# Seven block products for units 2 to 7 of a first expert stage, and another way to turn float64 words into float32

## The chip, the cores and the metric

The kernel runs on one core of a Trainium2 chip. A core has TensorE for matrix products, VectorE, ScalarE and GpSimd for work on elements, and SyncE, which issues most transfers. The profile calls them PE (its weight loads PEld), DVE, ACT, POOL and SP. The metric is device time in microseconds (us), the median of several runs.

## The reference, cut to what matters

Attention with a bias of position gives 1152 tokens of 512 features. A feed-forward stage with softplus follows, and then a stage of eight experts, each weighted by a column of P, a matrix that is balanced eight times by rows and columns.

```
x = attention(q, k, v, w1, b1, w2)              # 1152 x 512
h = x @ w_in                                    # 512 x 2048
g = max(h, 0) + log1p(exp(-abs(h)))             # softplus
x = g @ w_out                                   # 2048 x 512
P = exp(x @ w_gate - max); 8 times: rows, columns normalised
for e in range(8):
    out += P[:, e:e+1] * (max(x @ w1[e], 0) @ w2[e])   # 512 x 1024, 1024 x 512
```

`w_in` and `w_out` come as float64, the other inputs as float32.

## The kernel before, in words

**Stages.** First the bias is built, then attention runs (to about 262 us of the profile), and then `experts` handles both expert stages as 40 units of 256 hidden columns. Units 0 to 7 (U1 = 8) are the softplus stage, called the first expert stage here. Units 8 to 39 are the eight experts, four units each. Tokens are cut into two chunks of 512 and a rest of 128 (CHUNKS). Each float32 operand is split into a high part (rounded to the type that TensorE multiplies, by ScalarE) and a low part (source minus high, by VectorE or GpSimd), and each product is three products, high with high, high with low, low with high (TRIPS). In the text the low part is called a low.

**A unit.** Up products make h for chunk c and half f of the hidden columns, h(c,f). A *plain* unit makes four of them, each with four slices of the 512 features, 12 matmuls, 48 in all (`plain`). A unit with *seven block products* takes the two chunks by two halves of the features as a 2 x 2 matrix of blocks A11 to A22, the weights as another, and makes the four results from seven products of sums of blocks (PRODUCTS: S1 to S4 are sums of token blocks, T1 to T4 of weight blocks), six matmuls each, 42 in all (`product`). The products are accumulated in three PSUM banks X, Y and Z (tags t, tail, pv); between products the banks are copied to SBUF (v1, u2, u3, by `keep` on ScalarE) and added (`add` on VectorE). The T blocks are mixed from the weights by `mix`, four subtractions on GpSimd (L633 to L636). The order of the products is UP = 1, 2, 6, 5, 7, 3, 4, and last the rest of the tokens (`up_last`). Before the change units 0 to 8 are plain and units 9 to 39 use seven products.

After the up products come softplus or relu and the split of h, then `down(u, 0)` and `down(u, 1)`, four groups of six matmuls each into two PSUM tiles `sum` of two banks (the groups 0 and 2 share one tile, 1 and 3 the other), `turn_last` (two transposes and a split, hl) and `down_last`, six matmuls for the rest of the tokens into bank pv. Each group is added into acc by `evac` (L835 on VectorE; in unit 0 a copy by ScalarE, L833). acc takes the same SBUF places as the tokens xr of the first stage.

**Weights.** A unit has four pieces of 128 x 512 words: k = 0, 1 of `w_in`, k = 2, 3 of `w_out`. Those of units 0 to 7 are float64 and are turned into float32 while the unit before runs: `m` (mask on VectorE, L604, clamp on GpSimd, L605, a tensor_scalar with max and min), `a` (shift and mask, L610), `b` (or in the bits of the low word, L615) and `c` (or in the sign, L621), the last three on VectorE. `high` and `highd` split the finished weights into wu and wd (ScalarE L639, 1024 columns, GpSimd L640). A list of steps CONVERT, written by hand, sets the order; `convert(n)` takes the next n steps of it, two after each up product and one after each group of down. The pieces of units 0 and 1 are loaded, and those of unit 0 converted, during attention (EARLY).

**Order.** Nothing is scheduled: each engine executes its instructions in the order of the program text, and waits at one hold up all behind it on that engine. Ahead of unit 0, `x_part` splits the last block A22 (L662 on ScalarE, L663 on GpSimd and VectorE) and `x_last` splits the rest of the tokens (xl). In unit 8, which is plain, the logits of the gate are made in bank pv (`logits`) and turned into rows there (`tokens_down`), with `gate` as the table of what is asked for at which point.

## Time and profile before

| | us |
|---|---|
| median of three runs | 1245.1 (1243.65 to 1245.86) |
| the profiled execution | 1242.65 |
| its span | 1240.9 |
| PE busy | 1187.5 (96%) |
| DVE busy | 758.0 (61%) |
| POOL busy | 553.9 (45%) |
| ACT busy | 530.3 (43%) |
| share of PE in the chain that ended last | 81% |
| share of DVE in that chain | 10% |

The busy time of TensorE is the share of the span in which a matmul was in the pipeline. The chain that ended last is followed back from the last instruction; 81% of it is TensorE, so most of what is saved or added there shows in the time. Times in the rows are from the start of the span. A row of a timeline has start, duration, engine, line, operation and result<-operands, and in brackets how long the engine was idle before it and for whom it waited.

### The profile page before, as it was taken

What the parts mean: (1) busy time and instruction counts of PE and PEld (TensorE: products, weight loads), DVE (VectorE), ACT (ScalarE), POOL (GpSimd) and SP (SyncE); (2) the same over time, 40 slices, a digit from 0 to 9 for tenths busy, and PEclk for the clock granted to TensorE, in tenths of its full rate; (3) what the DMA queues carried; (4) which work ended last, traced back from release to release, by engine and by line L of the source; (5) the groups of instructions that cost most, each with busy time, mean ns of one, the idle gap of its engine ahead of it and who ended that gap; (6) DMA issues with size and microseconds to landing.
All of it is one profiled execution on the core that took longest, in us unless ns stands there. A gap on an engine that the chain in (4) does not pass through costs nothing.

```text
span 1240.9 us, 18958 instructions
## 1 busy us (share of the span) xinstructions
PE 1187.5 (96%) x7454; PEld 1003.3 (81%) x7454; DVE 758.0 (61%) x1393; ACT 530.3 (43%) x923; POOL 553.9 (45%) x424
## 2 busy tenths in 40 slices
PE   5877899999999999999999999999999999999998
PEld 4776788878788887888888888888888888888887
DVE  8985778746776757466554554554554554555554
ACT  7976676765223334423523323323323423422421
POOL 0115677655445544534543543543543453453440
PEclk9898999999999999999999999999999999999999
DMA  3577565312222310101111111110111111111102
GB/s 102 170 209 202 169 193 167 94 35 85 85 86 85 102 53 33 52 35 35 52 51 35 51 51 34 52 52 35 51 51 34 52 52 35 51 51 35 34 1 77
DMA packets 58572, 90.85 MB, mean 73 GB/s; under 512 B 6900, under 2 KB 37236, under 8 KB 58484
## 3 DMA queue, kind: packets, MB, share of 16 engines
q1 hardware_dynamic: 58196, 89.35, 22.9%
q8 instruction: 58, 0.95, 0.3%
q10 hardware_dynamic: 288, 0.30, 0.1%
q14 instruction: 30, 0.25, 0.1%
HBM read 74.45 MB, written 15.19 MB: 72 GB/s over the span
## 4 chain that ended last, share of the span: by engine, by line
PE 81%; DVE 10%; ACT 3%; POOL 3%; DMA 2%; issue 2%; SPq 0%; POOLq 0%; DVEq 0%; ACTq 0%
PE sum L802 34%; PE t L705 14%; PE pv L705 7%; PE pv L818 4%; PE t L721 4%; PE tail L776 4%; PE tail L705 3%; PE op L474 3%; PE sps L386 2%; PE pv L721 2%; PE tail L721 2%; PE tp L437 2%; ACT m L199 1%; DVE m L202 1%; DVE f L610 1%
## 5 line engine op out<-in xcount | busy, mean ns | idle before, releaser
L640 POOL TENSOR_TENSOR wu<-f,wu 128x1024 fp32r<-128x1024 f32 x71 | 170.6, 2403 | 436.0 <-ACT wu L639 436.0
L802 PE MATMUL sum<-wd,h 128*128 128x512 f32 x1536 | 364.9, 393 | 0.0
L802 PEld LDWEIGHTS sum<-wd,h 128*128 128x128 f32 x1536 | 283.3, 188 | 56.1
L837 DVE SCALAR_TENSOR_TENSOR acc<-sum,prob,acc 128x512 f32<-128x512 f32 x224 | 168.2, 751 | 146.7 <-PE sum L802 146.7
L705 PE MATMUL t<-room,wu 128*128 128x512 f32 x496 | 137.8, 389 | 0.0
L731 ACT ACTIVATE v<-t 128x512 f32<-128x512 f32 x31 | 18.5, 597 | 232.7 <-PE t L705 232.7
L640 POOL TENSOR_TENSOR wd<-f,wd 128x1024 fp32r<-128x1024 f32 x40 | 96.2, 2406 | 40.8 <-ACT wd L639 32.6
L705 PEld LDWEIGHTS t<-room,wu 128*128 128x128 f32 x496 | 93.1, 188 | 19.5
L802 PE MATMUL sum<-h,wd 128*128 128x512 f32 x384 | 93.9, 397 | 1.7 <-DVE acc L835 1.0
L705 PE MATMUL pv<-x,wu 128*128 128x512 f32 x372 | 94.8, 390 | 0.0
L212 PE MATMUL pac<-bw,m 128*128 128x64 bf16 (+1 forms) x1920 | 69.3, 201 | 26.4 <-ACT m L199 13.4
L212 PEld LDWEIGHTS <-m 128*128 128x128 bf16 (+1 forms) x1920 | 66.0, 107 | 29.6 <-issue 16.9
L802 PEld LDWEIGHTS sum<-h,wd 128*128 128x128 f32 x384 | 69.9, 188 | 20.5 <-DVE acc L835 5.8
L639 ACT ACTIVATE wu<-f 128x1024 fp32r<-128x1024 f32 x71 | 74.7, 1053 | 15.3 <-DVE f L621 15.3
L705 PEld LDWEIGHTS pv<-x,wu 128*128 128x128 f32 x372 | 69.6, 188 | 14.4
L747 ACT ACTIVATE hl<-tail 128x256 fp32r<-128x256 f32 x40 | 15.3, 383 | 143.7 <-PE tail L785 143.7
L605 POOL TENSOR_SCALAR f<-f 128x512 f32<-128x512 f32 x32 | 61.6, 1934 | 27.8 <-DVE f L604 27.3
L705 PE MATMUL t<-x,wu 128*128 128x512 f32 x248 | 71.3, 389 | 0.0
L835 DVE TENSOR_TENSOR acc<-sum,acc 128x512 f32<-128x512 f32 x80 | 55.0, 688 | 24.3 <-PE sum L802 23.5
L403 ACT ACTIVATE p<-p,sm 128x576 f32<-128x576 f32 x72 | 55.6, 773 | 21.6 <-DVE sm L399 17.7
L726 DVE TENSOR_TENSOR tail<-tail,v 128x512 f32<-128x512 f32 x31 | 21.7, 699 | 68.7 <-PE tail L705 68.7
L639 ACT ACTIVATE wd<-f 128x1024 fp32r<-128x1024 f32 x40 | 42.1, 1053 | 47.4 <-DVE f L621 47.4
(197 smaller groups left out, 2121.8 us busy)
## 6 DMA issues: line engine op xcount, KB each, us to landing
f<-in_e_w_dram SPq DMA_DIRECT2D x128, 256.0 KB, 2.8
bias<-wt SPq DMA_DIRECT2D x16, 576.0 KB, 5.8
raw<-in_w_in_dram SPq DMA_DIRECT2D x16, 512.0 KB, 3.6
raw<-in_w_out_dram SPq DMA_DIRECT2D x16, 512.0 KB, 3.6
wt<-extra SPq DMA_DIRECT2D x10, 512.0 KB, 4.6
raw<-in_qT_dram SPq DMA_DIRECT2D x16, 288.0 KB, 4.4
raw<-in_kT_dram SPq DMA_DIRECT2D x16, 288.0 KB, 4.4
vr<-in_vN_dram SPq DMA_DIRECT2D x8, 448.0 KB, 4.9
```

Source lines behind the costliest of these rows:

```text
L212: nc.tensor.matmul(pt[0:n, g], lhs, win(w, (k * (ng + 1) + gw) * NC, [[(ng - gw) * NC, 2], [1, NC]]), start=(k == 0), stop=(k == 2))
L403: nc.scalar.activation(p, p, AF.Exp, bias=sm[:, o:o + 1], scale=-1.0, accum_out=sm[:, 2 + o:3 + o])
L605: nc.gpsimd.tensor_scalar(t, t, F64_MIN, F64_MAX, ALU.max, ALU.min)
L639: nc.scalar.activation(w[:, 0], src, AF.Copy)
L640: nc.gpsimd.tensor_tensor(out=w[:, 1], in0=src, in1=w[:, 0].bitcast(F32), op=ALU.subtract)
L705: nc.tensor.matmul(zz, wu(u)[:, a, o:o + 128], xs[xn][b][j], start=(n in (1, 2, 5) and k == 0), stop=(k == 5), skip_group_check=True)
L721: nc.tensor.matmul(zz, wu(u)[:, a, o:o + 128], xs[f"A{c + 1}{k // 2 + 1}"][b][k % 2], start=(k == 0 and n == 0), stop=(k == 3 and n == 2))
L776: nc.tensor.matmul(zr[:, 0:256], xl[:, b, k], wu(u)[:, a, 256 * k:256 * k + 256], start=(n == 0), stop=(n == 3 * KT - 1))
L802: nc.tensor.matmul(s, lhs, rhs, start=(n == 0), stop=(n == 5))
L818: nc.tensor.matmul(r, t[:, b, 128 * f:128 * f + 128], w[:, a, f], start=(n == 0), stop=(n == 5))
L835: nc.vector.tensor_tensor(out=d, in0=o, in1=d, op=ALU.add)
L837: nc.vector.scalar_tensor_tensor(out=d, in0=o, scalar=pool["prob"][:, t, e:e + 1], in1=d, op0=ALU.mult, op1=ALU.add)
```

## The change

Units 2 to 7 use seven block products (PLAIN). Their h goes through SBUF: `add` writes v1, u2 or u3, softplus is made in place on ScalarE, and three of four lows are GpSimd subtractions, held back until the product after next for two of them (`held`). The T blocks need `mix` and a second `high` for each of these units, which CONVERT now holds; `highd` is made in its own unit, after the fourth product. S1 to S4 are made in unit 0 on VectorE (`first_sum`, eight additions) and split in units 0 and 1 (`first_split`). The conversion steps of unit 1 move from unit 0's up products to its down products.

Step `m` becomes two scalings by powers of two, one on ScalarE (`rescale`, L602 after) and two multiplications on GpSimd (L603); the masks of steps `a` and `c` change by a bit. Both lows of A22 are made on VectorE. `tokens_down` uses bank tail, and three entries of `gate` are asked for one step later.

```diff
-        PLAIN = tuple(range(U1 + 1))
+        PLAIN = (0, 1, U1)
...
 
-        def magnitude(u, k):
+        def rescale(u, k):
 
             if u < U1 and wide:
                 t = whole(u, k)
-                nc.vector.tensor_scalar(t.bitcast(I32), words(u, k)[:, :, 1], 0x7FFFFFFF, None, ALU.bitwise_and)
-                nc.gpsimd.tensor_scalar(t, t, F64_MIN, F64_MAX, ALU.max, ALU.min)
+                nc.scalar.activation(t, words(u, k)[:, :, 1].bitcast(F32), AF.Copy, scale=2.0**111)
+                nc.gpsimd.tensor_scalar(t, t, 2.0**-112, 2.0**-111, ALU.mult, ALU.mult)
 
         def convert_a(u, k):
             if u < U1 and wide:
                 t = whole(u, k).bitcast(I32)
-                nc.vector.tensor_scalar(t, t, 3, 0x3FFFFFFF, ALU.logical_shift_left, ALU.bitwise_and)
+                nc.vector.tensor_scalar(t, t, 3, 0x7FFFFFFF, ALU.logical_shift_left, ALU.bitwise_and)
 
         def convert_b(u, k):
             if u < U1 and wide:
@@ -618,7 +616,7 @@
         def convert_c(u, k):
             if u < U1 and wide:
                 t, w = whole(u, k).bitcast(I32), words(u, k)
-                nc.vector.scalar_tensor_tensor(out=t, in0=w[:, :, 1], scalar=-0x40000000, in1=t, op0=ALU.bitwise_and,
+                nc.vector.scalar_tensor_tensor(out=t, in0=w[:, :, 1], scalar=-0x80000000, in1=t, op0=ALU.bitwise_and,
                                                op1=ALU.bitwise_or)
 
...
-        def add(bank_, name):
-            out = hold[name if name == "u3" else bank_]
+        def add(u, bank_, name):
+            out = hold[bank_ if u >= U1 and name != "u3" else name]
             nc.vector.tensor_tensor(out=out, in0=hold[bank_], in1=hold[name], op=ALU.add)
             return out
...
-        def split_h(u, t, src):
+        def split_h(u, t, src, eng=None):
             nc.scalar.activation(t[:, 0], src, AF.Copy if u < U1 else AF.Relu)
-            if u < U1:
+            if eng:
+                eng.tensor_tensor(out=t[:, 1], in0=src, in1=t[:, 0].bitcast(F32), op=ALU.subtract)
+            elif u < U1:
                 lows.append(lambda: nc.vector.tensor_tensor(out=t[:, 1], in0=src, in1=t[:, 0].bitcast(F32), op=ALU.subtract))
             else:
...
-            while held:
-                held.pop(0)()
+            if n in (6, 4):
+                while held:
+                    held.pop(0)()
             if n in (2, 7, 3, 4):
                 c, f = {2: (0, 0), 7: (1, 1), 3: (0, 1), 4: (1, 0)}[n]
-                z[c, f] = hold["X"] if n == 4 else add(*{2: ("Y", "v1"), 7: ("X", "u3"), 3: ("Z", "u2")}[n])
+                z[c, f] = hold["X"] if n == 4 else add(u, *{2: ("Y", "v1"), 7: ("X", "u3"), 3: ("Z", "u2")}[n])
                 low()
-                act(u, c, f, z[c, f])
+                if u >= U1:
+                    act(u, c, f, z[c, f])
+                    return
+                if n == 4:
+                    z[c, f] = pool["moe"].tile([128, 512], F32, tag="s3", bufs=1, name="s3")
+                t = h[c, f] = pool["moe"].tile([128, 2, 512], F32R, tag="h", bufs=4, name="h")
+
+                def rest_of():
+                    nc.scalar.activation(z[c, f], hold["X"] if n == 4 else z[c, f], AF.Softplus)
+                    split_h(u, t, z[c, f], None if n == 3 else nc.gpsimd)
+
+                if n in (2, 7):
+                    held.append(rest_of)
+                else:
+                    rest_of()
                 return
...
-                convert(1)
+                convert(1 if u or c else (3, 3, 2, 1)[k])
...
-            lt, m = bank("pv"), CHUNKS[c][1] // 128
+            lt, m = bank("tail"), CHUNKS[c][1] // 128
...
-        gate = {(0, "a0"): lambda: (tokens_down(1), splits("S3")), (0, "a2"): lambda: logits(2), (0, "b0"): tokens_max,
+        gate = {(0, "a1"): lambda: (tokens_down(1), splits("S3")), (0, "a3"): lambda: logits(2), (0, "b1"): tokens_max,
...
-        CONVERT = "m0 m1 a0 b0 c0 m2 a1 b1 c1 high0 a2 b2 m3 c2 a3 b3 c3 highd0".split()
+        CONVERT0 = "m0 m1 a0 b0 c0 m2 a1 b1 c1 a2 high0 b2 m3 c2 a3 b3 c3".split()
+        CONVERT = "m0 m1 a0 b0 c0 m2 a1 b1 c1 high0 mix0 a2 b2 m3 c2 a3 high1 b3 c3".split()
...
-            x_part("A22", 0)
-            x_part("A22", 1, nc.vector)
+            for k in range(2):
+                x_part("A22", k, nc.vector)
...
                 if u + 1 < U1:
-                    todo.extend((u + 1, x[:-1], int(x[-1])) for x in CONVERT)
-                for n, (c, f) in enumerate(((0, 0), (0, 1), (1, 0), (1, 1))):
-                    do(u, (c, f))
+                    todo.extend((u + 1, x[:-1], int(x[-1])) for x in (CONVERT if u else CONVERT0))
+                if u == 0:
+                    first_plain()
+                elif u in PLAIN:
+                    for n, (c, f) in enumerate(((0, 0), (0, 1), (1, 0), (1, 1))):
+                        do(u, (c, f))
+                        low()
+                        act(u, c, f, z[c, f])
+                        if n == 1:
+                            weights["highd"](u, 0)
+                            first_split("S4")
+                        convert(2)
+                        jobs(n)
+                    up_last(u)
                     low()
-                    act(u, c, f, z[c, f])
-                    convert(2)
-                    jobs(n)
-                up_last(u)
-                low()
+                else:
+                    for n, p in enumerate(UP):
+                        if p:
+                            do(u, p)
+                        else:
+                            up_last(u)
+                        if n == 3:
+                            weights["highd"](u, 0)
+                        if n % 2:
+                            convert(2)
+                        jobs(n)
+                    low()
...
                 down(u, 1)
+                if u == 0:
+                    first_split("S2")
                 convert(len(todo))
+                if u == 1:
+                    first_split("S3", nc.vector)
                 down_last(u)
...
+        def first_plain():
+
+            def up(c, f):
+                do(0, (c, f))
+                low()
+                act(0, c, f, z[c, f])
+
+            tmp = [pool["moe"].tile([128, 512], F32, tag=t, bufs=1, name=t) for t in ("v1", "u2", "u3", "s3")]
+            pool["tmp"] = dict(S1=tmp[0:2], S2=[fs[1][:, 0:512], fs[1][:, 512:1024]], S3=tmp[2:4], S4=tmp[0:2])
+            up(0, 0)
+            first_sum("S1")
+            low()
+            first_sum("S2")
+            up(0, 1)
+            first_split("S1")
+            low()
+            first_sum("S3")
+            up(1, 0)
+            first_sum("S4")
+            up(1, 1)
+            low()
+            up_last(0)
+
+        def first_sum(name):
+            t = pool["tmp"]
+            for k in range(2):
+                a, b, op = {"S1": (x_of("A21"), x_of("A22"), ALU.add), "S2": (t["S1"], x_of("A11"), ALU.subtract),
+                            "S3": (x_of("A11"), x_of("A21"), ALU.subtract), "S4": (x_of("A12"), t["S2"], ALU.subtract)}[name]
+                nc.vector.tensor_tensor(out=t[name][k], in0=a[k], in1=b[k], op=op)
+
+        def first_split(name, eng=nc.gpsimd):
+            for k in range(2):
+                hi, lo, src = xs[name][0][k], xs[name][1][k], pool["tmp"][name][k]
+                nc.scalar.activation(hi, src, AF.Copy)
+                eng.tensor_tensor(out=lo, in0=src, in1=hi.bitcast(F32), op=ALU.subtract)
```

**Unit 0, VectorE.** The instructions after the last copies of attention (po<-tps). Before, the low of A22, then conversions and lows of h:

```order
L423 COPY po<-tps 128x320
L663 TENSOR_TENSOR x_4613<-xr,room 128x512
L604 TENSOR_SCALAR f_4602<-raw_2557 128x512
L604 TENSOR_SCALAR f_4602<-raw_2558 128x512
L749 TENSOR_TENSOR h<-z,h 128x512
L610 TENSOR_SCALAR f_4602<-f_4602 128x512
L615 SCALAR_TENSOR_TENSOR f_4602<-raw_2557,f_4602 128x512
L749 TENSOR_TENSOR h<-z,h 128x512
```

After:

```order
L421 COPY po<-tps 128x320
L661 TENSOR_TENSOR x_4613<-xr,room 128x512 x2
L1214 TENSOR_TENSOR v_4629<-xr 128x512
L1214 TENSOR_TENSOR u_4630<-xr 128x512
L749 TENSOR_TENSOR h<-z,h 128x512
L1214 TENSOR_TENSOR f_2556<-v_4629,xr 128x512
L1214 TENSOR_TENSOR f_2556<-u_4630,xr 128x512
L749 TENSOR_TENSOR h<-z,h 128x512
L1214 TENSOR_TENSOR u_4631<-xr 128x512
L1214 TENSOR_TENSOR s_4632<-xr 128x512
L1214 TENSOR_TENSOR v_4629<-xr,f_2556 128x512
L1214 TENSOR_TENSOR u_4630<-xr,f_2556 128x512
```

Eight sums (L1214) stand where the conversions of unit 1 stood, and the last two of them read xr.

**Unit 0, ScalarE.** From gl, the softplus of the rest of the tokens, on. Before:

```order
L780 ACTIVATE gl<-t 128x256
L833 ACTIVATE acc<-sum 128x512 x2
L639 ACTIVATE wu_4600<-f_4602 128x1024
L833 ACTIVATE acc<-sum 128x512 x2
L747 ACTIVATE hl<-tail 128x256
```

After:

```order
L795 ACTIVATE gl<-t 128x256
L848 ACTIVATE acc<-sum 128x512
L602 ACTIVATE f_4602<-raw_2557 128x512
L602 ACTIVATE f_4602<-raw_2558 128x512
L848 ACTIVATE acc<-sum 128x512
L602 ACTIVATE f_4604<-raw_4605 128x512
L848 ACTIVATE acc<-sum 128x512 x2
L745 ACTIVATE hl<-tail 128x256
```

Three rescales stand between the copies of sum into acc, and the high part of wu has moved behind them.

**A unit of the middle, GpSimd.** One unit's worth of instructions while the next one's weights are converted. Before:

```order
L605 TENSOR_SCALAR f_4602<-f_4602 128x512 x2
L605 TENSOR_SCALAR f_4604<-f_4604 128x512
L640 TENSOR_TENSOR wu_4600<-f_4602,wu_4600 128x1024
L605 TENSOR_SCALAR f_4604<-f_4604 128x512
L640 TENSOR_TENSOR wd_4601<-f_4604,wd_4601 128x1024
```

After, without the first two rescales:

```order
L747 TENSOR_TENSOR h<-v_5410,h 128x512
L638 TENSOR_TENSOR wd_2554<-f_4603,wd_2554 128x1024
L603 TENSOR_SCALAR f_4604<-f_4604 128x512
L747 TENSOR_TENSOR h<-u_5443,h 128x512
L747 TENSOR_TENSOR h<-s_5480,h 128x512
L638 TENSOR_TENSOR wu_4600<-f_4602,wu_4600 128x1024
L631 TENSOR_TENSOR f_2556<-f_4602 128x2x2x128
L632 TENSOR_TENSOR f_2556<-f_4602 128x2x128
L633 TENSOR_TENSOR f_2556<-f_4602,f_2556 128x2x128
L634 TENSOR_TENSOR f_2556<-f_2556 128x2x128
L603 TENSOR_SCALAR f_4604<-f_4604 128x512
L638 TENSOR_TENSOR wu_4600<-f_2556,wu_4600 128x1024
```

Three lows of h, the four subtractions of the mix and a second low of wu have come in.

**The same unit's end, VectorE.** From the third group of the second half of down on. Before:

```order
L610 TENSOR_SCALAR f_4603<-f_4603 128x512
L835 TENSOR_TENSOR acc<-sum,acc 128x512
L615 SCALAR_TENSOR_TENSOR f_4603<-raw_4606,f_4603 128x512
L621 SCALAR_TENSOR_TENSOR f_4603<-raw_4606,f_4603 128x512
L835 TENSOR_TENSOR acc<-pv,acc 128x512
L604 TENSOR_SCALAR f_4602<-raw_2557 128x512
L604 TENSOR_SCALAR f_4602<-raw_2558 128x512
L749 TENSOR_TENSOR h<-t,h 128x512
```

After:

```order
L850 TENSOR_TENSOR acc<-sum,acc 128x512
L608 TENSOR_SCALAR f_4603<-f_4603 128x512
L613 SCALAR_TENSOR_TENSOR f_4603<-raw_4606,f_4603 128x512
L619 SCALAR_TENSOR_TENSOR f_4603<-raw_4606,f_4603 128x512
L850 TENSOR_TENSOR acc<-pv,acc 128x512
L724 TENSOR_TENSOR v_5800<-tail,v_5800 128x512
L608 TENSOR_SCALAR f_4602<-f_4602 128x512
L613 SCALAR_TENSOR_TENSOR f_4602<-raw_2557,f_4602 128x512
```

The whole of the fourth piece's steps a, b and c now stands between the last addition from sum and the addition from pv, and the next unit's first addition of products (L724) behind them.

## Rows read from the trace of the kernel before

**Rows 1.** Windows of stretches: length, busy of each engine (instructions), clock, DMA.

```profile
core 0: us, PE busy (x) PEld busy (x) DVE busy (x) ACT busy (x) POOL busy (x), PEclk, DMA share, GB/s
261.27:295.31 34.04, 31.91 (x151) 25.43 (x149) 16.51 (x30) 18.15 (x36) 19.21 (x15) 1.00 0.23 77
295.31:320.76 25.45, 25.30 (x117) 20.60 (x116) 16.99 (x27) 7.72 (x13) 12.40 (x6) 1.00 0.25 81
320.76:346.30 25.54, 25.33 (x118) 20.64 (x117) 18.68 (x31) 7.62 (x12) 12.40 (x6) 1.00 0.27 83
448.40:473.34 24.94, 24.94 (x118) 20.68 (x117) 11.92 (x19) 13.09 (x21) 16.43 (x11) 1.00 0.19 63
473.34:506.44 33.10, 31.33 (x154) 23.60 (x153) 19.90 (x35) 15.51 (x27) 10.73 (x8) 1.00 0.10 32
603.24:626.71 23.47, 23.47 (x112) 19.63 (x110) 12.31 (x17) 7.75 (x12) 10.49 (x7) 1.00 0.14 45
```

**Rows 2.** Timeline of TensorE: down in unit 4, products in the second stage.

```profile
391.55 4.59 PE L802 MATMUL sum<-h,wd 128*128 128x512 f32 x18 [0.20 <-DVE acc L835]
...
603.24 1.52 PE L705 MATMUL t<-room,wu 128*128 128x512 f32 x6
604.60 1.52 PE L705 MATMUL tail<-room,wu 128*128 128x512 f32 x6
```

**Rows 3.** Timeline of VectorE and GpSimd in unit 5, down.

```profile
413.76 2.40 POOL L640 TENSOR_TENSOR wu<-f,wu 128x1024 fp32r<-128x1024 f32 x1 [4.66 <-ACT wu L639]
...
414.56 1.88 DVE L610 TENSOR_SCALAR f<-f 128x512 int32<-128x512 int32 x1
416.36 0.68 DVE L835 TENSOR_TENSOR acc<-sum,acc 128x512 f32<-128x512 f32 x1
...
420.95 0.43 DVE L610 TENSOR_SCALAR f<-f 128x512 int32<-128x512 int32 x1
```

**Rows 4.** Timeline of GpSimd and VectorE, a little later.

```profile
419.00 1.92 POOL L605 TENSOR_SCALAR f<-f 128x512 f32<-128x512 f32 x1 [2.83 <-DVE f L604]
...
419.43 0.72 DVE L621 SCALAR_TENSOR_TENSOR f<-raw,f 128x512 int32<-128x512 int32 x1
```

**Rows 5.** Timeline of GpSimd and VectorE in attention.

```profile
122.44 2.82 POOL L334 TENSOR_TENSOR ql<-raw,qh 128x576 fp32r<-128x576 f32 x2 [1.13 <-PE sps L386]
...
143.36 3.25 POOL L334 TENSOR_TENSOR ql<-raw,qh 128x576 fp32r<-128x576 f32 x2 [1.57 <-PE sps L386]
...
144.07 1.26 DVE L615 SCALAR_TENSOR_TENSOR f<-raw,f 128x512 int32<-128x512 int32 x1
```

**Rows 6.** Groups by line: count | busy us, mean ns of one | idle before, releasers.

```profile
L640 POOL TENSOR_TENSOR wu<-f,wu 128x1024 fp32r<-128x1024 f32 x71 | 170.6, 2403 | 436.0 <-ACT wu L639 436.0
L605 POOL TENSOR_SCALAR f<-f 128x512 f32<-128x512 f32 x32 | 61.6, 1934 | 27.8 <-DVE f L604 27.3
L633 POOL TENSOR_TENSOR f<-f 128x512 f32<-128x512 f32 x31 | 40.0, 1292 | 0.0
L413 POOL TENSOR_SCALAR p<-p,sm 128x576 f32<-128x576 f32 x48 | 39.3, 820 | 31.9 <-DVE sm L409 18.5 <-PE tp L437 6.4 <-DVE vx L295 4.0
L636 POOL TENSOR_TENSOR f<-f 128x256 f32<-128x256 f32 x31 | 22.9, 738 | 0.0
L663 POOL TENSOR_TENSOR room<-xr,room 128x512 fp32r<-128x512 f32 x6 | 7.7, 1286 | 3.0 <-ACT room L662 2.9
...
L639 ACT ACTIVATE wu<-f 128x1024 fp32r<-128x1024 f32 x71 | 74.7, 1053 | 15.3 <-DVE f L621 15.3
L747 ACT ACTIVATE h<-t 128x512 fp32r<-128x512 f32 x49 | 29.4, 599 | 8.4 <-PE t L721 7.8 <-PE t L705 0.2
```

**Rows 7.** Timeline of TensorE: three of its waits.

```profile
138.43 0.66 PE L437 MATMUL tp<-ident,p 128*128 128x128 f32 x4 [2.48 <-POOL p L413]
...
288.38 1.88 PE L802 MATMUL sum<-h,wd 128*128 128x512 f32 x7 [0.36 <-ACT acc L833]
...
488.12 1.09 PE L898 MATMUL pv<-room,gw 128*16 128x512 f32 x4 [0.84 <-DVE prob L910]
```

**Rows 8.** Timeline of VectorE ahead of unit 0.

```profile
275.41 1.34 DVE L663 TENSOR_TENSOR x<-xr,room 128x512 fp32r<-128x512 f32 x1 [7.91 <-ACT room L662]
```

More of the change, by code (lines that the diff above doesn't have):

```diff
@@ L52 @@
 STEP_SCALE = float(2.0**30)
-F64_MIN = float(np.array([0x38000000], np.uint32).view(np.float32)[0])
-F64_MAX = float(np.array([0x47EFFFFF], np.uint32).view(np.float32)[0])
 VROW = 256 + 512 + 128
@@ L648, in highd @@
                 parts(wd(u), whole2(u, 1))
-        weights = dict(m=magnitude, a=convert_a, b=convert_b, c=convert_c, mix=lambda u, k: mix(u), high=high, highd=highd)
+        weights = dict(m=rescale, a=convert_a, b=convert_b, c=convert_c, mix=lambda u, k: mix(u), high=high, highd=highd)
         xs = {}
@@ L1013, in beside @@
             for n, at in enumerate(EARLY):
-                for k, fn in enumerate((load, magnitude, convert_a, convert_b)):
+                for k, fn in enumerate((load, rescale, convert_a, convert_b)):
                     if k < len(at) and s == at[k]:
```

## The prediction

> **What bounds the kernel now.** I read the busy times by stretch first. In the first expert stage, about 295 to 473 us, TensorE is busy for all but 0.2 us of each 25.5 us unit, with VectorE at about 18.7 and GpSimd at 12.4 [rows 1]. A unit of the second stage, which has seven block products instead of a plain product, takes 23.47 us and no wait. The last plain unit (448.40 to 473.34) has no conversion of a next unit beside it and takes 24.94; units 2 to 6 take 25.5. So 0.60 us of a unit is a wait that the conversions cause, and 24.94 - 23.47 = 1.47 is work that seven products save (six matmuls of 0.227 are 1.36; a group of six follows the last after 1.36 [rows 2]).
>
> The wait of 0.60 is seen next. In the second half of a unit TensorE stops for an addition into acc (L835) [rows 2]. VectorE has done the shift of a conversion (L610) just ahead of it: 1.88 us instead of the 0.43 that it takes elsewhere, ending 0.28 after GpSimd's subtraction (413.76 + 2.40 = 416.16; 414.56 + 1.88 = 416.44) [rows 3]. So VectorE's instruction waits for GpSimd's. The addition, which reads PSUM, keeps its 0.68. Three more rows bound this. A GpSimd tensor_scalar with max and min (L605, 1.92 us) did not hold up L621, which took 0.72 inside it [rows 4]. Two GpSimd subtractions in a row took 3.25 us with a two-operand VectorE instruction waiting, 2.82 without. That instruction ended at 145.33, about 0.56 after the first subtraction's end (143.36 + 1.41), and the second ran after it [rows 5]: they take turns. I call what they take turns on the port.
>
> The Trainium skill, "SBUF — State Buffer", section "SBUF: two separate sides", says that VectorE and GpSimd share a port pair which one instruction holds to its end while the other engine waits. It speaks against this change, which gives GpSimd more to do. The trace agrees for GpSimd's subtractions, not for L605.
>
> **Attention, about 105 to 261 us.** Four float64 pieces are converted here. VectorE loses four masks, ScalarE gets four rescales of about 0.60 (nearest row, L747; ScalarE's read at a step of two words is not shown: 0.60 to twice that), and GpSimd's clamp L605 of 1.93 becomes two multiplications. For these L413, also two multiplications, is nearest: 0.82 on 576 columns, 0.73 on 512 [rows 6]. One clamp stands ahead of the L413 on which TensorE waits 2.48 us [rows 7]; there up to 1.2 us go. The four ScalarE instructions cost at most 2.4 if all hit the chain. I take -1.0, bounds -3 and +2.
>
> **Unit 0.** VectorE now has two lows of A22, eight sums L1214 and two lows of h ahead of everything else, twelve instructions of 0.69 (SBUF operands, as L621), starting about 0.5 us earlier than the L663 of before (275.41) since it needs not wait for GpSimd's [rows 8]: 274.9 + 8.3 = 283.2. Five of them meet a GpSimd subtraction, three lows of xl (128 columns each, at most a L636 of 0.74) and two lows of S1 of 1.29 [rows 6]; I put these waits at 2.8 (estimate), so the last sum S4 ends at 286.0. That matters because acc[0] takes the place of xr[0], which S4 reads: the first copy of sum into acc waits for it. ScalarE has behind it, in this order, that copy, m0, m1, the second copy, m2 and the third: six of 0.60, to 289.65. The second half's first product needs the third copy, as at 288.38 now [rows 7]. So it starts 1.3 us later: **+1.3**. In its favour TensorE itself would be there by 286.7, since the A22 low on VectorE shortens an earlier wait. Bounds -1.7 (the waits hidden) and +2.7 (they double).
>
> **Unit 1**, still plain, no longer has a shift ahead of an addition that TensorE waits for: after the change the three additions stand together and the shift behind them. 25.45 becomes 24.94 [rows 1]: -0.5, bounds -0.5 and +1.
>
> **Units 2 to 7.** They take 152.58 us now (320.76 to 473.34) [rows 1], and 6 x 23.47 = 140.82 if TensorE never waits. GpSimd's queue of a unit grows to three subtractions of 2.40, three lows of h of 1.29, a mix of 1.29 + 3 x 0.74 = 3.51 and four rescales of 0.73, together 17.5 us [rows 6]; its tail lies in line with VectorE's. I laid out one unit from its first product, with TensorE in groups of 1.36. The first product of the first half ends at 12.3. The piece c1 stands behind the low of h(1,1) on GpSimd (its high part leaves ScalarE at 12.0, a VectorE instruction is ahead, so 12.6 to 13.9) and ends 0.56 later, at 14.45. From there every step waits for the last: GpSimd's low of h(1,0) (1.29) to 15.75, beside which ScalarE makes the high part (1.05); the low of wu (2.40) 18.15; the shift a2 (0.28) 18.43; the mix, with b2 and c2 taking turns at 0.56, 23.05; m3 (0.73) 23.78; a3 (0.43) 24.2; the low of the mixed weights (2.40) 26.6; b3 (0.56), c3 (0.69) and the addition of the last rows from bank pv (0.68) **28.5**. The next unit starts at 23.47 and its fourth product, four groups on, begins bank pv anew: 27.55. It would wait 0.97. If b3 goes before GpSimd instead, the mixed weights land late for the third product and the wait is of the same size. Everything after it moves by the same amount, so the wait comes once a unit and does not grow. Unit 2 follows unit 1, whose chain has more room, and gets none: five waits, 4.85 us. 140.82 + 4.85 = 145.67, against 152.58: **-6.9**. Bounds: -11.8 with no wait, and the rival on the port below. The additions of products (three, 0.69, one operand in PSUM), the three copies v1, u2, u3 and the softplus passes are nothing on the path: VectorE reaches them within the 1.36 of the next product, and ScalarE has some 13 us of 0.38 to 1.05 us passes in a unit of 24. Without that cover each would cost its 0.6 to 0.7. The loads on SP keep their order; the raw buffers come free with c0 and c1, more than 10 us ahead of use.
>
> **Unit 8.** The 33.10 us hold 1.77 of TensorE idle time [rows 1], 0.84 of it for the logits' bank pv, which tokens_down has not read yet [rows 7]. tokens_down gets bank tail and is asked for one step later; both waits go. -1.75, bounds -1.8 and 0.
>
> **Sum.** -1.0 + 1.3 - 0.5 - 6.9 - 1.75 = -8.85. The profiled execution took 1242.65 us (span 1240.9), so its like would take 1233.8; the median of the three runs is 1245.1, 2.45 above it, and I predict against the median: 1236.2 (own range 1232 to 1241).
>
> **Rivals.**
> *No waiting.* VectorE's tail ends before 27.55, as when c1 is 1 us earlier. Units 2 to 7 give -11.8 and the sum -13.7: 1231.4. For it: only 1 us has to be found. Against it: the chain leaves no gap to find it in.
>
> *The port is the bound.* Each instruction keeps the other engine out for its whole time, even a rescale. The Trainium skill's page "SBUF — State Buffer" (section "Who interferes with whom") makes the lock exclusive in that way. GpSimd's 17.5 and VectorE's 4 x 0.43 + 9 x 0.69 = 7.9 add to 25.4 us, above the 23.47 of TensorE. Units 2 to 6 would take 25.4, unit 7, which converts nothing, 24.4: 151.4, or -1.2, and the sum -3.15: 1241.95. For it: rows 3 and 5. Against it: after a wait VectorE needs only 0.28 or 0.56, and rows 4.
>
> *GpSimd keeps the port through a run of instructions (slower).* In unit 0 the sums would wait out the four xl lows and both S1 lows (+2.7 in all instead of +1.3). In a product unit a2 waits for the low of wu and the whole mix, from 18.2 to 24; the low of hl stands behind a2 and the last rows' product waits for it, 1.5 us in each of six units, 1 in unit 1, and bank pv comes 1.2 late five times: 140.82 + 9 + 6 = 155.8, or +3.2. In attention the conversions wait out pairs of subtractions (+1.3 twice): +1.6. Sum 1.6 + 2.7 + 1.0 + 3.2 - 1.75 = +6.8: 1251.9. It decides from waits of 2 us a unit on. Against it: rows 5, where they take turns.
>
> *The change does not do what it says* (the last of the six units still plain, or the clamp still paid): order and diff say otherwise; it would end near 1244.
>
> **Chances.** Forecast 0.50, no waiting 0.15, port 0.20, run of instructions 0.12, nothing done 0.03. A change of 0.2% (2.5 us) is about what can be told from none. Faster: 0.49 + 0.15 + 0.12 (about six tenths of the port case) = 0.76; slower 0.12; same 0.12. The range goes from below no waiting, 1229 with attention at its better end, to 1244; it leaves out the slow rival and some ends, under 2 in 10.
>
> **What would show it.** Windows of units 3 to 6 at 24.4 us; a TensorE wait of about 1 us before the fourth product in each, put down to VectorE's addition from pv; the rescale on GpSimd at 0.7; shifts of 1 us and more wherever a subtraction runs; the second half of unit 0 waiting for ScalarE's acc; no wait at the logits. Units at 23.5 mean no waiting, at 25.4 the port. A rescale near 1.9 us, or units above 25.5, make the prediction wrong.

## The result, and the profile after the change

The changed kernel takes 1232.5 us (median of 4 runs, 1231.0 to 1233.1) against 1244.8 for the kernel before (4 runs, 1243.7 to 1245.9): a ratio of 0.990, interval 0.9883 to 0.9917. The forecast was 1236.2, own range 1232 to 1241; the rival of no waiting gave 1231.4, so by the time alone the result lies nearer to it. The profiled execution after took 1233.1 us with a span of 1231.3, 9.6 us less than the span before; it is at the slow end of its four, and the profiled one before (1242.65) was faster than all four of its own, so the medians lie further apart, 12.3 us.

Windows of the changed kernel: units 0, 1, 2, 4, 7 and 8 (same columns as [rows 1]).

```profile
core 0: us, PE busy (x) PEld busy (x) DVE busy (x) ACT busy (x) POOL busy (x), PEclk, DMA share, GB/s
260.24:293.79 33.55, 31.91 (x151) 25.33 (x149) 19.41 (x30) 20.83 (x42) 15.64 (x15) 1.00 0.21 71
293.79:318.65 24.86, 24.86 (x118) 20.68 (x116) 20.07 (x26) 13.97 (x24) 18.97 (x17) 1.00 0.24 76
318.65:344.41 25.76, 23.77 (x112) 19.55 (x110) 21.46 (x29) 12.80 (x21) 19.12 (x15) 1.00 0.25 83
368.71:392.32 23.61, 23.61 (x111) 19.55 (x110) 19.41 (x28) 12.34 (x20) 19.07 (x15) 1.00 0.29 92
440.02:464.77 24.75, 23.97 (x111) 19.39 (x110) 16.01 (x19) 14.62 (x24) 22.96 (x15) 1.00 0.20 65
464.77:496.55 31.78, 31.09 (x154) 23.63 (x153) 19.95 (x35) 15.42 (x27) 10.95 (x8) 1.00 0.10 34
```

A unit with seven block products has 112 matmuls where a plain one has 118, and GpSimd is busy for 19.1 us of it (12.4 before). Units 3, 5 and 6, not shown, take 24.30, 24.12 and 23.58. So units 2 to 7 take 146.12 us (before 152.58), and they are not alike: unit 4 has no wait, unit 2 has one of 1.99. TensorE's waits answer [rows 7]; its timeline, three places:

```profile
135.68 0.66 PE L435 MATMUL tp<-ident,p 128*128 128x128 f32 x4 [0.29 <-POOL p L411]
...
324.88 1.66 PE L703 MATMUL pv<-x,wu 128*128 128x512 f32 x6 [1.99 <-DVE acc L850]
...
452.95 1.43 PE L817 MATMUL sum<-h,wd 128*128 128x512 f32 x5 [0.78 <-DVE h L749]
```

The wait of 2.48 in attention is 0.29 now, the logits' wait of 0.84 is gone, and the two others are new. What VectorE did ahead of the first of them (its timeline, to be read beside GpSimd's low of the mixed weights, L638, from 318.04 to 320.44):

```profile
318.09 2.63 DVE L608 TENSOR_SCALAR f<-f 128x512 int32<-128x512 int32 x1
320.76 0.69 DVE L613 SCALAR_TENSOR_TENSOR f<-raw,f 128x512 int32<-128x512 int32 x1
321.48 1.12 DVE L619 SCALAR_TENSOR_TENSOR f<-raw,f 128x512 int32<-128x512 int32 x1
322.53 1.09 DVE L1220 TENSOR_TENSOR room<-u,room 128x512 fp32r<-128x512 f32 x1
323.55 0.68 DVE L1220 TENSOR_TENSOR room<-s,room 128x512 fp32r<-128x512 f32 x1
324.15 0.68 DVE L850 TENSOR_TENSOR acc<-pv,acc 128x512 f32<-128x512 f32 x1
```

The shift of the fourth piece is held until 0.28 after GpSimd's subtraction, as in [rows 3]; behind it stand the low bits, the sign, S3's two subtractions, and only then the addition that empties bank pv.

### The profile page after: what moved, and what is told of

The parts are those of the page before. It is cut to its first block, busy times and chain, and to the rows that moved or that the text cites. A ratio compares the mean times of both kernels' runs of the same rounds, so it can differ in the third digit from the quotient of the medians.

```text
span 1231.3 us, 19016 instructions
## 1 busy us (share of the span) xinstructions
PE 1179.1 (96%) x7418; PEld 996.8 (81%) x7418; DVE 774.1 (63%) x1372; ACT 567.7 (46%) x987; POOL 591.5 (48%) x477
## 4 chain that ended last, share of the span: by engine, by line
PE 84%; DVE 9%; ACT 3%; issue 1%; DMA 1%; POOL 1%; SPq 0%; DVEq 0%; POOLq 0%; ACTq 0%
PE sum L817 36%; PE t L703 15%; PE pv L703 8%; PE tail L791 4%; PE pv L833 4%; PE tail L703 4%; PE op L472 3%; PE sps L384 2%; PE tp L435 2%; PE t L719 1%; ACT m L197 1%; DVE m L200 1%; PE pac L210 1%; DVE extra L234 1%; DMA raw<-in_kT_dram 1%
## 5 line engine op out<-in xcount | busy, mean ns | idle before, releaser
L638 POOL TENSOR_TENSOR wu<-f,wu 128x1024 fp32r<-128x1024 f32 x77 | 186.3, 2419 | 410.1 <-ACT wu L637 409.3
L703 PE MATMUL t<-room,wu 128*128 128x512 f32 x592 | 164.5, 389 | 0.0
L729 ACT ACTIVATE v<-t 128x512 f32<-128x512 f32 x37 | 22.2, 599 | 244.6 <-PE t L703 244.6
L703 PEld LDWEIGHTS t<-room,wu 128*128 128x128 f32 x592 | 111.1, 188 | 23.5 <-DVE u L724 0.3
L703 PE MATMUL pv<-x,wu 128*128 128x512 f32 x444 | 113.8, 392 | 2.5 <-DVE acc L850 2.4
L638 POOL TENSOR_TENSOR wd<-f,wd 128x1024 fp32r<-128x1024 f32 x40 | 96.5, 2414 | 11.3 <-ACT wd L637 10.5
L703 PEld LDWEIGHTS pv<-x,wu 128*128 128x128 f32 x444 | 82.6, 188 | 21.5 <-DVE acc L850 4.2
L637 ACT ACTIVATE wu<-f 128x1024 fp32r<-128x1024 f32 x77 | 81.0, 1053 | 29.9 <-POOL f L634 23.8
L703 PE MATMUL t<-x,wu 128*128 128x512 f32 x296 | 85.1, 389 | 0.0
L724 DVE TENSOR_TENSOR u<-t,u 128x512 f32<-128x512 f32 x37 | 25.6, 692 | 72.4 <-PE t L703 69.8
L850 DVE TENSOR_TENSOR acc<-sum,acc 128x512 f32<-128x512 f32 x80 | 55.0, 688 | 22.9 <-PE sum L817 22.1
L703 PEld LDWEIGHTS t<-x,wu 128*128 128x128 f32 x296 | 55.6, 188 | 11.5
L724 DVE TENSOR_TENSOR tail<-tail,v 128x512 f32<-128x512 f32 x31 | 21.7, 700 | 67.7 <-PE tail L703 67.7
```

Source lines behind the costliest of these rows:

```text
L637: nc.scalar.activation(w[:, 0], src, AF.Copy)
L638: nc.gpsimd.tensor_tensor(out=w[:, 1], in0=src, in1=w[:, 0].bitcast(F32), op=ALU.subtract)
L703: nc.tensor.matmul(zz, wu(u)[:, a, o:o + 128], xs[xn][b][j], start=(n in (1, 2, 5) and k == 0), stop=(k == 5), skip_group_check=True)
L724: nc.vector.tensor_tensor(out=out, in0=hold[bank_], in1=hold[name], op=ALU.add)
L850: nc.vector.tensor_tensor(out=d, in0=o, in1=d, op=ALU.add)
```

## The experiments

Each edit is made to the changed kernel. Unit lengths are from one profiled execution each; where nothing was edited they repeat to 0.2 us, but for unit 3 (24.3 us in three traces, 23.6 in e7) and for the clock (last section).

**e1_clamp: the old conversion.**

```diff
-nc.scalar.activation(t, words(u, k)[:, :, 1].bitcast(F32), AF.Copy, scale=2.0**111)
-nc.gpsimd.tensor_scalar(t, t, 2.0**-112, 2.0**-111, ALU.mult, ALU.mult)
+nc.vector.tensor_scalar(t.bitcast(I32), words(u, k)[:, :, 1], 0x7FFFFFFF, None, ALU.bitwise_and)
+nc.gpsimd.tensor_scalar(t, t, F64_MIN, F64_MAX, ALU.max, ALU.min)
...                                             # the masks of steps a and c as before
```

> The changed kernel with the old conversion put back (mask on VectorE, clamp with max and min on GpSimd), everything else as changed. Theory A (conversions lie in line with the additions that TensorE waits for): each clamp takes 1.93 us where the two multiplications took 0.7 to 1.1, at least the one of the fourth piece stands in line, so the wait ahead of the fourth product is 0.9 to 1.5 us in each of units 2 to 7 and these units take 150 to 154 us in place of 146.1; attention gives back the 1.0 that it had gained. Together 5 to 9 us longer than the changed kernel. Theory B (GpSimd's conversions are hidden under TensorE, only attention felt the clamp): units 2 to 7 stay within 1 us of 146.1, attention +1.0, about 1 to 2 us in all.

Measured: 1268.5 us, 1.0196 of before (1.018 to 1.0212), 36 us above the changed kernel where theory A had 5 to 9. Units 2 to 7 take 171.0 us: theory B falls, and theory A is right in kind and far too small. Unit 1, which is plain, takes 30.92 where it took 24.86, and 25.45 before the change; the stretch from 105 us to unit 0 takes 5.3 more. Unit 4 in windows, the clamp's group, and one of the held masks:

```profile
387.91:416.18 28.27, 25.49 (x111) 19.08 (x110) 23.75 (x30) 10.21 (x16) 24.51 (x15) 1.00 0.24 75
```

```profile
L605 POOL TENSOR_SCALAR f<-f 128x512 f32<-128x512 f32 x32 | 67.2, 2105 | 26.8 <-DVE f L604 26.5
```

```profile
400.17 2.62 DVE L604 TENSOR_SCALAR f<-raw 128x512 int32<-128x512 int32 x1
```

GpSimd alone is busy for 24.5 us, more than TensorE needs, and waits for masks that its own subtractions hold. So the changed kernel's order with the old conversion is slower than the kernel before. Since the plain unit 1 suffers too, this is not the seven products alone; no run has them with the old conversion in an order made for it.

**e9_mask and e10_clampact: the old conversion in halves** (the first line above, then the second, changed alone, the clamp with other bounds).

> The changed kernel with one half of the old conversion back: the first step is the mask on VectorE in place of ScalarE's rescale, GpSimd's two multiplications stay (the exponents of the converted weights then come out wrong; that part of the computation is left out). It and the next run split the 24.9 us that the whole old conversion costs in units 2 to 7. Theory A (GpSimd's clamp is the price): units 2 to 7 take 146 to 149 us. Theory B (VectorE's extra instruction, held by GpSimd's subtractions, is the price): 154 to 162.

> The other half: ScalarE's rescale stays, GpSimd does a tensor_scalar with max and min again (with bounds that keep the numbers finite; the values of the weights are left out). Theory A (GpSimd's clamp, four of about 1.1 us more, makes its queue of 19 us as long as a unit): units 2 to 7 take 156 to 168 us, with waits put down to GpSimd or to additions behind held steps. Theory B (VectorE's mask is the price): 146 to 150.

Measured: units 2 to 7 take 154.35 with the mask and 161.79 with the clamp, 8.2 and 15.7 us above 146.12; the sum, 23.9, is nearly the 24.9 of both. So each half costs by itself, and the clamp is two thirds of it. GpSimd's group L603 of the clamp run:

```profile
L603 POOL TENSOR_SCALAR f<-f 128x512 f32<-128x512 f32 x32 | 68.3, 2142 | 9.4 <-ACT f L602 9.4
```

In the changed kernel the same group has a mean of 824 ns, on the same tile: 32 x 1.32 = 42 us of GpSimd.

**e2_plain: eight chunks again.** `PLAIN = tuple(range(U1 + 1))`, and the split of S4 stays in unit 1 alone. Units 2 to 7 there multiply S3, which lies in A21's place, so their values are others; the work is that of plain units.

> The changed kernel with units 2 to 7 plain again (eight chunks of products in place of seven), all else as changed. Theory A (the seven products save TensorE's work, the new conversion only takes away the wait of 0.6): units 2 to 7 take 24.94 to 25.1 each, 149.7 to 150.6 in all, 3.5 to 4.5 us longer than in the changed kernel. Theory B (the wait of 0.6 stays in plain units whatever the conversion): 152.6 in all, 6.5 longer. Below 149.6 neither holds, since TensorE alone takes 24.94 for a plain unit.

Measured: 1236.2 us (0.9937, interval 0.9918 to 0.9956). Units 2 to 6 take 24.83 each without a wait, unit 7 24.93, 149.09 in all. Theory A in kind; the sum lies under the 149.6 that was named as the least, because a plain unit takes 24.83 here and not the 24.94 of unit 7 before. Of the 6.46 us that units 2 to 7 gained, the new conversion and its order bring 152.58 - 149.09 = 3.49, and the seven products 2.97 more.

**e3_gate: bank and order of the logits as before.**

> The changed kernel with tokens_down back in bank pv and at its old places in unit 8. Theory A (the bank and the order of the logits were the waits): unit 8 takes 33.0 to 33.5 us in place of 31.78, with a wait of about 0.8 us at the logits again, and nothing else moves. Theory B (unit 8 gained because its inputs come earlier): unit 8 stays at 31.8.

Measured: unit 8 takes 33.16 in place of 31.78, with waits of 0.9 at L913 and 0.9 at L920 (in the changed kernel none, and 0.7). Theory A; unit 2 is longer too, by its clock (last section).

**e4_tail: the addition from pv first.**

```diff
+down_last(u)
 convert(len(todo))
-down_last(u)
-CONVERT = "... m3 c2 a3 high1 b3 c3"
+CONVERT = "... m3 c2 high1 a3 b3 c3"
```

> The changed kernel with the last three conversion steps of a unit (shift, low bits and sign of its fourth piece, which only the next unit's highd needs) behind the addition of the last rows on VectorE, for units 1 to 6. Theory A (the wait ahead of the fourth product is that addition standing in VectorE's queue behind conversions that GpSimd holds up): the waits put down to L850 (1.99 in unit 2, 0.39 in unit 3) go or fall to under 0.2, units 2 and 3 take 23.6 to 24.0, units 4 to 6 stay within 0.3, so 2 to 3 us less than the changed kernel. Theory B (the product is late because the weights or the last rows' product are late): the wait stays at 1.5 to 2 us in unit 2 and units 2 to 7 at 146.

Measured: 1231.3 us; units 2 to 7 take 144.68, units 2 and 3 25.13 and 23.60. No wait is put down to L850 any more, so theory A holds for the cause. But 1.4 us came back, not 2 to 3. In unit 2 a wait of 1.24 stands two groups later, for ScalarE's copy L729:

```profile
326.01 1.65 PE L703 MATMUL pv<-x,wu 128*128 128x512 f32 x6 [1.24 <-ACT u L729]
```

VectorE's first addition of products now stands behind the held steps, and ScalarE's copy of u behind the softplus that needs it.

**e8_s3: S3's split earlier on VectorE**, ahead of unit 1's second product.

> The changed kernel with the split of S3 ahead of the second half of unit 1's second product in place of behind it; VectorE then has no S3 between the shift of the fourth piece and the addition from pv. Theory A (S3's two subtractions, 1.1 + 0.7, are most of unit 2's wait of 1.99): that wait falls to 0.2 to 0.6, unit 2 takes 24.0 to 24.4 in place of 25.76, unit 1 stays within 0.4 of 24.86. Theory B (the wait is the shift held for 2.63 by GpSimd, and S3 fills a hole): the wait stays above 1.3.

Measured: unit 2 takes 23.51, but unit 1 takes 27.10, with a wait of 1.89 for an addition into acc: 50.61 for the two in place of 50.62. Theory A is right for unit 2, wrong for the whole: held by the mix in its new place, the same two subtractions took 1.45 and 1.21, and the additions behind them were waited for there.

**e5_extra and e6_tail_extra: 2.4 us more on GpSimd**, in the old order and in e4's.

> The changed kernel with the low part of the mixed weights made twice on GpSimd, 2.4 us more of GpSimd in each of units 1 to 6 (its result is the same). Theory A (the tail of GpSimd's queue stands in line with VectorE's last conversions and the addition from pv): the extra holds up the low bits or the sign of the fourth piece, the wait ahead of the fourth product grows by 2.1 to 2.4 in units 2 to 7, and these take 158 to 161 us in place of 146.1. Theory B (GpSimd's tail is hidden, only the order on VectorE counts): 146 to 148.

> The same extra in the kernel that has the last three conversion steps behind the addition from pv (units 2 to 7 took 144.7 there). Theory A: the addition is no longer held, but the three steps now stand ahead of the first addition of products (L724), which had 0.5 us to spare; with a held step ending some 1.9 us later about 1.3 us come back in each unit, as a wait for ScalarE's copy u: units 2 to 7 take 150 to 153, 6 to 9 less than with the extra in the old order, and no wait is put down to L850. Theory B (GpSimd's busy time itself is the bound, 19 + 2.4 us and the turns): 158 to 161 in both orders.

Measured: 162.82 and 158.49, both above what theory A gave for them. The edit was a poor one: TensorE's third product also waits for the extra subtraction, since it writes weights (0.9 to 1.6 a unit with the old order, 1.2 to 1.3 with e4's), so no size can be read from it. The two orders lie 4.3 us apart, some of which is a lower clock after two of e5's waits and one of e6's (last section). With the addition ahead the waits for L850 are gone (6.3 us in three of the six units with the old order). What the tail of GpSimd's queue costs by itself stays open.

**e7_s4late: unit 0's sums.** The two sums S3 are made three times ahead of S4.

> The changed kernel with the two sums S3 made three times in unit 0, so that the sum S4 behind them ends some 2.7 us later (near 286.8 where unit 0 starts at 260.2). Theory A (as predicted: the first copy into acc takes the place of what S4 reads and waits for it): the first copy starts only then, 3.8 us later than 22.75 us into the unit, and the unit takes 36.5 to 37.5 us in place of 33.55. Theory B (only the columns that S4 reads are held, the third and fourth copy): the first copy stays at 22.75 us into the unit, the third waits for S4, and the unit takes 33.8 to 34.6, some of it for the lows of h that stand behind S4.

Measured: unit 0 takes 37.33. VectorE, then ScalarE, then TensorE:

```profile
284.34 0.68 DVE L1216 TENSOR_TENSOR s<-xr 128x512 f32<-128x512 f32 x1
284.94 0.68 DVE L1216 TENSOR_TENSOR v<-xr,f 128x512 f32<-128x512 f32 x1
285.55 0.68 DVE L1216 TENSOR_TENSOR u<-xr,f 128x512 f32<-128x512 f32 x1
```

```profile
285.13 0.60 ACT L848 ACTIVATE acc<-sum 128x512 f32<-128x512 f32 x1 [3.11 <-DVE s L1216]
```

```profile
285.78 4.61 PE L817 MATMUL sum<-h,wd 128*128 128x512 f32 x12 [3.11 <-ACT acc L848]
```

The time is theory A's, the cause is neither's: the first copy starts 0.11 after S3's last sum (285.02) and 1.1 before the end of S4's (286.23). S3 reads the first two pieces of xr[0], S4 the last two. The copy writes only the first; why it waits for the sum that reads the second is not shown. Of the 3.78 us, 2.44 are the later copy (25.19 us into the unit in place of 22.75); the rest is TensorE's clock (last section).

**e11_best and e12_final: the waits taken away together.** Both have e4's order and S3's split on GpSimd in unit 1, ahead of the first product of down, where GpSimd waited 2.5 us. They differ in two small pieces.

```diff
-first_split("S3", nc.vector)          # behind unit 1's conversions
+first_split("S3")                     # ahead of down(1, 0), on GpSimd
 FIRST = {1: (("high", 0),), 3: (("highd", 0),)}    # e11: 8 for 3; e12: 7 for 3
 gate_split()     # end of unit 4; e11: end of unit 6; e12: in unit 7, behind the second group
```

> The changed kernel with four small moves: the last three conversion steps of a unit behind the addition from pv; the split of S3 on GpSimd ahead of unit 1's second product, where GpSimd waits 2.5 us; the parts of unit 8's second weights (highd) after unit 7's first half instead of right behind those of unit 7; the gate's split in unit 7, which converts nothing. Theory A (the waits left come from the order on VectorE and GpSimd): unit 2 takes 23.5 to 24.0, unit 5 23.6, unit 7 23.6 to 24.2, units 2 to 7 together 141.5 to 143.0, 3 to 4.5 us less than the changed kernel, 1228 to 1229.5. Theory B (a wait that is taken away in one place comes back in the next, as S3's did in unit 1): 144 to 146.

> The changed kernel with the moves that the run before bore out (last three conversion steps behind the addition from pv, S3's split on GpSimd in unit 1), the gate's split in unit 7 where VectorE and GpSimd both have a pause (behind the first addition of products, 3 us in), and highd of unit 8 behind the last rows of unit 7's up products. Theory A (each of these two small pieces only cost because it met a GpSimd subtraction): units 2 to 6 take 23.5 each, unit 7 23.5 to 24.0, units 2 to 7 together 141.2 to 141.8, some 4.5 us less than in the changed kernel; unit 1 keeps 25.2; the whole 1228 to 1230. Theory B (unit 7's load on GpSimd comes back elsewhere in it): unit 7 at 24.5 or more, the six at 142.2 or more.

Measured: in e11 units 2 to 6 take 23.52 or 23.53 each, but unit 7 takes 26.41, so 144.04 in all: theory A for five units, B for the sixth and for the sum. The whole takes 1232.2 us (0.9905, interval 0.9888 to 0.9921), where 1228 to 1229.5 was expected. In unit 7 TensorE waits 1.56 for a copy behind VectorE's first addition of products and 0.75 for an addition into acc. Ahead of the first stands the gate's cast of 128x32, which takes 0.59 in the changed kernel and was here held by the low of unit 8's weights:

```profile
441.46 2.38 DVE L904 CAST gw<-graw 128x32 fp32r<-128x32 f32 x1
```

In e12 unit 7 takes 23.58 and units 2 to 7 take 141.03, theory A and a little under its range: TensorE does not wait in any of them. Against e2's 149.09 the seven products bring 8.06 there (if plain units take the same in this order, which was not run), where they brought 2.97 in the changed kernel. Units 2 and 7 of e12:

```profile
317.67:341.15 23.48, 23.48 (x111) 19.63 (x110) 18.79 (x26) 12.36 (x20) 19.29 (x15) 1.00 0.30 91
435.12:458.70 23.58, 23.58 (x112) 19.55 (x110) 15.48 (x22) 14.44 (x24) 20.16 (x12) 1.00 0.20 69
```

e12 takes 1229.9 us (1226.7 to 1231.3; 0.988 of before, interval 0.9863 to 0.9898), 5.1 less than the changed kernel in units 2 to 7 and 0.4 more in unit 1. Its median is the lowest of all, but its interval and the changed kernel's overlap: attention alone varies by 4 us from execution to execution (next section).

## Why the prediction was right, and where it was not, step by step

The sum was -8.85 and the spans differ by -9.6. The rest of the 3.7 us between forecast and median is that the 2.45 by which the median before lay above its profiled run was carried over: after, the median lies 0.6 below it.

- **Attention, -1.0: -1.03 in the two traces, by luck** (from 105 us to unit 0: 156.27 and 155.24). The wait ahead of L413 fell as said, 2.48 to 0.29; with the clamp back (e1) it was 2.54 again. But from 112 us on the trace after has two stretches of low granted clock in attention, at 146 and at 221 us, each right behind a wait of 1.9, and the trace before has none. Here is the second, and below it the same place of e12, where the clock stayed (of each the wait, and a window with the columns of [rows 1]):

```profile
220.09 0.66 PE L435 MATMUL tp<-ident,p 128*128 128x128 f32 x4 [1.87 <-POOL p L411]
221.00:225.00 4.00, 4.00 (x17) 3.67 (x16) 1.88 (x7) 1.69 (x5) 1.43 (x3) 0.57 0.27 104
...
219.94 0.66 PE L435 MATMUL tp<-ident,p 128*128 128x128 f32 x4 [1.86 <-POOL p L411]
221.00:225.00 4.00, 4.00 (x31) 3.82 (x30) 3.44 (x10) 3.09 (x9) 1.40 (x4) 1.00 0.25 92
```

  Measured from the fifth of GpSimd's multiplications of p (118.50 before, 117.70 after) to unit 0, attention takes 142.8 before. In ten traces with the multiplications it takes 139.6 and 139.8 where there is no low stretch (e4, e12), 140.9 to 141.3 in four with one, 142.5 to 143.1 in four with two. So at an equal clock the change brings 3 us here, not 1, and a low stretch costs some 1.5. The term was too small, and the clock hid it in the one trace after. The medians, 12.3 apart, point the same way; of their executions there are no traces.
- **Unit 0, +1.3: -0.49.** This is the step that failed. The first copy into acc was to wait for S4; it waits for S3. The two sums S3, the last of S4, that copy, and TensorE's wait for it:

```profile
279.38 1.79 DVE L1214 TENSOR_TENSOR u<-xr 128x512 f32<-128x512 f32 x1
281.10 1.78 DVE L1214 TENSOR_TENSOR s<-xr 128x512 f32<-128x512 f32 x1
...
283.40 0.68 DVE L1214 TENSOR_TENSOR u<-xr,f 128x512 f32<-128x512 f32 x1
...
282.99 0.60 ACT L848 ACTIVATE acc<-sum 128x512 f32<-128x512 f32 x1 [0.70 <-PE sum L817]
...
283.64 3.27 PE L817 MATMUL sum<-h,wd 128*128 128x512 f32 x12 [0.69 <-ACT acc L848]
```

  S3 ends at 282.88 and the copy starts 0.11 later, before S4 ends at 284.08. (The profile names TensorE's sum, which ended a little later still; e7, with S3 alone 2.4 us later, shows that it is S3: the copy follows it by 0.11 again, and the unit is 3.8 longer.) The estimate of 2.8 us for turns was good: the five sums that took longer than 0.68 (0.95, 0.94, 0.77, 1.79, 1.78) hold 2.8 more together. S4 was laid out to end 24.73 us into the unit and ends 23.84 into it, since VectorE's steps follow each other by 0.60 where 0.69 was counted. The third copy ends 26.02 us into the unit in place of the 28.38 laid out, and the second half, 26.65 into it, waits for none. Beside one of 0.7 that both have, the waits of the unit are 0.29 and 0.69 in place of 0.91, 0.18 and 0.36.
- **Unit 1, -0.5: -0.59**, and e2 has 24.83 for the plain units 2 to 6: the wait of 0.60 went with the new conversion.
- **Units 2 to 7, -6.9: -6.46. The kind of wait was right; that the sum came out is luck.** The wait at the fourth product, put down to the addition from pv, came as forecast, and e4 shows that VectorE's order makes it. But it was to be 0.97 in each of units 3 to 7; it was 0.39 in unit 3 and nothing in 4 to 7, and units 4 and 6 (23.61, 23.58) are as the rival of no waiting has them. The six lie 5.3 above 140.82, where 4.85 was forecast; 4.2 of it stands in units 2, 5 and 7, for reasons that the forecast did not have (below). In unit 4 the chain ended 0.9 us sooner than the 28.5 laid out: the addition from pv ends 27.60 us into it, 0.09 before the next unit's fourth product starts:

```profile
395.63 0.68 DVE L850 TENSOR_TENSOR acc<-pv,acc 128x512 f32<-128x512 f32 x1
...
396.40 1.63 PE L703 MATMUL pv<-x,wu 128*128 128x512 f32 x6
```

  Turns cost GpSimd less than was said: the low of wu started 15.48 us into unit 4 and the mix ended at 21.87, where 15.75 and 23.05 were laid out:

```profile
384.19 2.41 POOL L638 TENSOR_TENSOR wu<-f,wu 128x1024 fp32r<-128x1024 f32 x1
386.55 1.50 POOL L631 TENSOR_TENSOR f<-f 128x512 f32<-128x512 f32 x1
388.00 1.19 POOL L632 TENSOR_TENSOR f<-f 128x256 f32<-128x256 f32 x1
389.14 0.74 POOL L633 TENSOR_TENSOR f<-f,f 128x256 f32<-128x256 f32 x1
389.85 0.73 POOL L634 TENSOR_TENSOR f<-f 128x256 f32<-128x256 f32 x1
390.55 1.07 POOL L603 TENSOR_SCALAR f<-f 128x512 f32<-128x512 f32 x1
391.76 2.68 POOL L638 TENSOR_TENSOR wu<-f,wu 128x1024 fp32r<-128x1024 f32 x1
```

  Alone the mix is 1.29 + 3 x 0.74 [rows 6]; only two of its four parts took a turn, at 0.2 and 0.45, where two of 0.56 were counted ([rows 5] themselves have 3.25 - 2.82 = 0.43), and the mix did not wait for the shift a2. m3, counted as 0.73, took 1.07. Three things were overlooked. Unit 2 was to have none, but S3's split, 1.8 us ahead of the addition, was left out of VectorE's queue there. In unit 5, 0.5 longer than 4 and 6, the gate's split of unit 4 (L904, L905) stands ahead of the first addition of products; moved away (e11) it leaves 23.53. In unit 7 two lows of wd stand in a row on GpSimd (4.76 from 447.59); the low of h on VectorE came due at 450.54, in the second, and took 2.36 instead of 0.69, to 0.55 after its end.
- **Unit 8, -1.75: -1.32.** Of its waits of 0.84 and 0.93, both counted as gone, the first went and the second is 0.69 now (L920, put down to ScalarE's copy); e3 brings both back. From unit 9 on the stage is 0.3 longer.

The rivals: the port as the bound gave 25.4 us a unit; e12's unit of 23.48 with 19.29 us of GpSimd and 18.79 of VectorE rules this price out. The Trainium skill, page "SBUF — State Buffer", section "Who interferes with whom", makes the lock exclusive. The trace agrees for the held steps above; it does not bear out the sum of full lengths, since the two engines' shares at their full lengths, 25.4 us, fitted into 23.48. The lengths are what was wrong: a held step is done 0.28 or 0.55 after GpSimd, and lengthens GpSimd's next by about 0.45. With the thirteen VectorE steps at 0.28 and 0.45 the same sum is 22.7 (an estimate). Against this rival the prediction also had rows 4, where a clamp did not hold VectorE, and took the rescale to be like it. It is not. In the changed kernel:

```profile
285.85 1.10 POOL L603 TENSOR_SCALAR f<-f 128x512 f32<-128x512 f32 x1 [0.39 <-ACT f L602]
286.50 0.99 DVE L619 SCALAR_TENSOR_TENSOR f<-raw,f 128x512 int32<-128x512 int32 x1
```

The step of VectorE takes 0.99 instead of 0.69 and ends 0.54 after the rescale. The trace before had shown it for L413, which also multiplies twice:

```profile
160.45 1.20 POOL L413 TENSOR_SCALAR p<-p,sm 128x576 f32<-128x576 f32 x1 [0.70 <-DVE vx L295]
161.08 1.11 DVE L621 SCALAR_TENSOR_TENSOR f<-raw,f 128x512 int32<-128x512 int32 x1
```

The run of instructions needed waits for whole runs, and none is seen: each held step shown here ends within 0.6 us of the end of the one GpSimd instruction that ran when it came due. No waiting came by itself in units 4 and 6, and in all six only with e12's order. Units 2 to 7 tell it from the forecast: 146.12, where the forecast had 145.67 and this rival 140.82.

## What to carry to other kernels

Lay the two engines' queues beside each other before moving work to GpSimd, and count from what each held instruction keeps behind it: an addition that empties a bank should stand ahead of conversions that nobody waits for yet (e4, e12). A stage's work can be replaced by less work only if the engine that feeds it has room: with the cheap conversion seven products brought 3 us in one order and 8 in another (149.09 in e2, 146.12 in the changed kernel, 141.03 in e12), and with the dear one the first of these orders took 171.0 (e1). A small instruction is priced by what it meets, not by its length: the same cast took 0.59 or 2.38, and S3's split cost as much in its new place as in its old one (e8). Look at the granted clock before two traces are compared: a stage that agrees with its forecast may do so only because the clock fell in one of them.

## What the runs showed of the hardware

- GpSimd's tensor_scalar on 128x512 takes 0.62 to 1.10 us with two multiplications and 1.91 to 2.42 with max and min, on the same tile in the same place (changed kernel and e10_clampact).
- The two also differ in what they do to VectorE. Of its steps with two operands in SBUF (low bits and sign, 128x512) that came due in units 0 to 8 while GpSimd multiplied twice (L603), all eight in the changed kernel were held and ended 0.54 us after it. In the kernel before, nineteen came due beside a clamp (L605), and each took 0.69 to 0.72 us, its usual time; in e1 and e10 some took 0.98, but none of these waited for the clamp's end.
- A wait of TensorE is sometimes followed by a lower granted clock. In e7, after 3.11 us of waiting, twelve matmuls took 4.61 us, where they take 3.27 in the changed kernel; the window of the wait and the one behind it:

```profile
279.77:285.78 6.01, 2.90 (x14) 2.07 (x12) 6.01 (x8) 2.84 (x7) 2.29 (x2) 1.00 0.00 0
285.78:290.40 4.62, 4.62 (x15) 3.69 (x15) 4.52 (x8) 2.75 (x5) 2.26 (x3) 0.63 0.00 0
```

  A clock of 0.63 is a stretch partly at the lower of the two levels (1.2 and 2.4 GHz). In e3 the same wait of 1.99 in unit 2 as in the changed kernel was followed by two groups of 2.40 and 2.41 instead of 1.66 and 1.52, and the unit took 27.42 in place of 25.76. In e5 six matmuls took 2.92 and 2.85 instead of 1.66 after waits of 2.59 and 2.72, in e6 2.08 after 1.84. In the changed kernel the clock stayed at 1.00 after the 1.99, and so it did in e1 after 3.01 us. Attention above shows the same: after a wait of 1.87 the clock fell, after 1.86 in the same place of another trace it did not. So the price of a wait is not only its length, and one trace does not tell it; what decides stays open.
